# Linear attention and two MLP layers on one core: attention by whole load groups, tail key products over 128 rows, rms_g inside the gate and value weights

## The chip, the cores and the metric

The kernel runs on one core of a Trainium2 chip. The metric is device time in microseconds (us), from the start of the execution to its end. One execution was also recorded by the hardware profiler; its span is the time from the first to the last instruction that the profiler saw. The engines are named as in the profile: PE is the matrix engine, PEld its weight loads, DVE the vector engine, ACT the scalar engine, POOL the GpSimd engine, and SP the engine that issues the transfers.

## The reference

Three layers follow one another. The inputs are four batches, eight heads, 576 positions of 64 values, 128 random features, and three weight pairs.

```python
scale = 1.0 / np.sqrt(np.sqrt(D))
def phi(x):
    proj = np.einsum('bhsd,md->bhsm', x, omega)
    sq = np.sum(x * x, axis=-1, keepdims=True) / 2.0
    h = proj - sq
    h = h - np.max(h, axis=-1, keepdims=True)
    return np.exp(h) / np.sqrt(m)
q_p, k_p = (phi(q * scale), phi(k * scale))
kv = np.einsum('bhsm,bhsd->bhmd', k_p, v)
z = np.sum(k_p, axis=2)
x = num / den                      # num = q_p @ kv, den = q_p @ z + 1e-6, as [2304, 512]

xn = x / np.sqrt(np.mean(x * x, -1, keepdims=True) + 1e-06) * rms_g
g = xn @ w_gate                    # 512 -> 1536
x = (g / (1 + np.exp(-g))) * (xn @ w_val) @ w_out

h = x @ w_in                       # 512 -> 2048
out = (h / (1 + np.exp(-h))) @ w2_out
```

## The kernel before

**Numbers in two parts.** Every product that needs more than one pass keeps its operands as a high and a low part, and adds three products (PASS). The weights arrive as 64-bit numbers: `w_decode` turns them into 32 bits, with five steps on DVE (lines 156 to 167) and two integer additions on POOL (line 170, `w_add`); ACT then writes the high part (line 180) and DVE the low one (line 183).

**Attention.** A load brings 256 positions of four heads (a "load group", `add_load`) or, for the last 64 positions of two batches together, one half-size tail group. POOL squares and halves it (lines 545, 549), and DVE reduces it to norms (line 558). A unit of work (`add_unit`) is half a load group, that is two heads, or one tail group: two 128x128 transposes on PE into half a PSUM bank (line 586), high part by ACT (592), low part by DVE (595), six products with omega of 256 columns each (605), the maxima on DVE (620), two small DVE instructions for the bias (626, 633), four exponentials on ACT (644). There are 64 half groups and 8 tail groups, 72 units in all. A key unit ends in eight products of 64 output rows by 65 columns into the accumulator `kv` (690). A tail group of keys holds two batches in its upper and lower 64 rows, so its products run over 64 rows, four of them at the end of the even batch and four at the end of the odd one. The finished `kv` is copied by DVE (710, `kvs`). A query unit ends in four transposes (721), a copy by ACT (727), eight products with `kvs` (736, for tails 742), and denominator, reciprocal and quotient on DVE (759, 762, 772).

**Norm and transposes.** For each 128 positions ACT sums squares (803), POOL takes the root (814, 817), DVE multiplies by it and by `rms_g` in one instruction (833, tile `g_sb`, a copy of the vector in every row), PE transposes (842), ACT and DVE split (851, 856) into the tile `xs`.

**What sets the order.** Everything up to the third block of tokens of the first sweep is planned by `run_order`: each step is an `Op` with engine, duration, wanted slots and a priority, to which the table `RANK` adds a number by kind; `SLOTS` gives the number of buffers. Slot kind `b` is six PSUM banks. The first sweep of the gated layer covers two of twelve feature blocks: its six weight tiles are gated by `pj_ops[24 + 2 * n]`, the projections of units 24 to 34, and its products are `part` (line 236) and `out` (963) for the first three blocks of 512 tokens. Three weight tiles of the second sweep also belong to the plan.

**The stream.** After the plan, `stream` writes the rest in a fixed order: products of gate and value (236, tile `g`), output products (290, 323, tile `y`). `Prep.tick` puts one weight load, the decoding of the weight loaded before, the high part of the one before that and the low part of the one before that between them, each time that 3.2 us (until the second sweep's weights are there), later 5.5 us, of PE work by its own count has been written.

## Time and profile before

| | before |
|---|---|
| median of three runs | 1011.57 us (1009.81 to 1011.66) |
| the profiled execution, its own time | 1011.63 us |
| its span | 1009.8 us |
| PE busy | 992.4 us (98%), granted clock 0.998 |
| DVE, ACT, POOL busy | 587.8, 374.6, 282.2 us (58%, 37%, 28%) |

The profiled execution is 0.06 us from the median; 1.83 us of its time lie outside the span. A busy PE need not be a PE at its peak: a matmul is counted from its start to its modelled end, and the next can start before that end. The share of DVE and ACT over the whole span hides that nearly all of attention lies in the first 167 us, where both are close to full.

### The profile page before, as it was taken

The numbers are of one execution on the slowest core, as the hardware profiler recorded it, in microseconds if no ns is written. First come the engines' busy times: TensorE is split into PE (matmuls) and PEld (weight loads), VectorE is DVE, ScalarE is ACT, GpSimd is POOL, SyncE is SP. The second block draws the span as 40 slices with busy tenths as digits, with TensorE's granted clock in tenths as the row PEclk, the third lists the DMA queues.
The fourth block names the chain that finished last, engine by engine and source line by source line (L and its number), as shares of the span: only waits on it lengthen the run. The fifth ranks groups of instructions, "written<-read, shape, count | busy, mean of one in ns | idle before, by whom it ended". The sixth has DMA issues, their size and how long they took to land.

```text
span 1009.8 us, 15330 instructions
## 1 busy us (share of the span) xinstructions
PE 992.4 (98%) x5935; PEld 842.4 (83%) x5935; DVE 587.8 (58%) x1289; ACT 374.6 (37%) x861; POOL 282.2 (28%) x287
## 2 busy tenths in 40 slices
PE   7999998999999999999999999999999999999998
PEld 7988886788888888888888888888888888888887
DVE  7899998837852345676332776443654544535633
ACT  6988895344221112222111334433322322322321
POOL 6756632415520002344000231321411411201300
PEclk9999999999999999999999999999999999999999
DMA  7444211212320002222000120210210210200023
GB/s 196 123 122 131 67 30 42 64 41 84 104 63 1 1 1 64 63 85 83 21 1 1 42 63 22 84 42 5 79 42 6 78 42 22 63 1 21 21 84 105
DMA packets 68729, 55.85 MB, mean 55 GB/s; under 512 B 25648, under 2 KB 62768, under 8 KB 68656
## 3 DMA queue, kind: packets, MB, share of 16 engines
q1 hardware_dynamic: 68656, 54.87, 18.4%
q8 instruction: 47, 0.77, 0.3%
q14 instruction: 26, 0.21, 0.1%
HBM read 50.14 MB, written 4.72 MB: 54 GB/s over the span
## 4 chain that ended last, share of the span: by engine, by line
PE 89%; DVE 7%; issue 1%; POOL 1%; ACT 1%; DMA 1%; SPq 0%; DVEq 0%; ACTq 0%; POOLq 0%
PE g L236 43%; PE y L323 19%; PE y L290 12%; PE b L605 4%; PE b L236 3%; PE kv L690 2%; DVE small L620 2%; PE b L963 2%; PE b L736 1%; PE b L721 1%; PE b L586 1%; DVE hl L595 1%; DVE w L183 1%; POOL m L170 1%; DVE xt L833 1%
## 5 line engine op out<-in xcount | busy, mean ns | idle before, releaser
L236 PE MATMUL g<-xs,w 128*128 128x512 f32 (+1 forms) x2256 | 467.9, 366 | 0.0
L236 PEld LDWEIGHTS g<-xs,w 128*128 128x128 f32 x2256 | 391.2, 188 | 70.1
L170 POOL TENSOR_TENSOR m<-m,raw 128x512 int32<-128x512 int32 x136 | 189.9, 1396 | 612.6 <-issue 442.6
L230 DVE TENSOR_TENSOR h<-s,h 128x512 fp32r<-128x512 f32 (+1 forms) x134 | 96.0, 717 | 185.0 <-ACT h L229 185.0
L323 PE MATMUL y<-w,h 128*128 128x512 f32 (+1 forms) x870 | 200.8, 388 | 0.0
L323 PEld LDWEIGHTS y<-w,h 128*128 128x128 f32 x870 | 162.2, 188 | 33.3
L229 ACT ACTIVATE h<-s 128x512 fp32r<-128x512 f32 (+1 forms) x134 | 78.7, 588 | 191.5 <-DVE s L259 169.5
L290 PE MATMUL y<-h,w 128*128 128x512 f32 (+1 forms) x648 | 135.6, 366 | 0.3 <-DVE w L183 0.3
L290 PEld LDWEIGHTS y<-h,w 128*128 128x128 f32 x648 | 112.1, 189 | 20.5 <-DVE w L183 0.8
L270 ACT ACTIVATE s<-g 128x512 f32<-128x512 f32 (+1 forms) x80 | 44.4, 556 | 171.0 <-PE g L236 170.9
L334 DVE TENSOR_TENSOR ya<-y,ya 128x512 f32<-128x512 f32 (+1 forms) x91 | 62.2, 684 | 57.8 <-PE y L323 56.5
L259 DVE TENSOR_TENSOR s<-s,g 128x512 f32<-128x512 f32 (+1 forms) x54 | 33.8, 627 | 84.8 <-PE g L236 84.8
L301 DVE TENSOR_TENSOR ya<-y,ya 128x512 f32<-128x512 f32 (+1 forms) x80 | 50.2, 635 | 54.3 <-PE y L290 54.1
L180 ACT ACTIVATE w<-m 128x512 fp32r<-128x512 f32 x68 | 42.7, 628 | 102.8 <-POOL m L170 102.8
L644 ACT ACTIVATE e<-b,nb 128x128 f32<-128x128 f32 x272 | 77.5, 395 | 3.7 <-DVE nb L633 3.6
L605 PE MATMUL b<-bd,hl 128*128 128x256 f32 x432 | 69.5, 300 | 1.7 <-DVE hl L595 1.1
L605 PEld LDWEIGHTS b<-bd,hl 128*128 128x128 f32 x432 | 56.8, 192 | 5.4 <-DVE hl L595 2.3
L620 DVE TENSOR_REDUCE small<-b 128x4 f32<-128x512 f32 x72 | 50.2, 697 | 6.2 <-PE b L605 2.2
L253 ACT ACTIVATE s<-g 128x512 f32<-128x512 f32 (+1 forms) x54 | 29.7, 550 | 64.1 <-PE g L236 63.9
L183 DVE TENSOR_TENSOR w<-m,w 128x512 fp32r<-128x512 f32 x68 | 52.9, 779 | 0.1
L545 POOL TENSOR_TENSOR sq<-x 128x512 f32<-128x512 f32 (+1 forms) x40 | 38.9, 982 | 36.2 <-DMA x<-in_q_dram 9.8
L549 POOL TENSOR_TENSOR sq<-sq 128x256 f32<-128x256 f32 (+2 forms) x80 | 44.4, 573 | 2.3
(69 smaller groups left out, 739.7 us busy)
## 6 DMA issues: line engine op xcount, KB each, us to landing
raw<-in_moe_w_out_dram SPq DMA_DIRECT2D x28, 512.0 KB, 3.5
raw<-in_moe_w_in_dram SPq DMA_DIRECT2D x16, 512.0 KB, 3.7
raw<-in_moe_w_gate_dram SPq DMA_DIRECT2D x12, 512.0 KB, 3.6
raw<-in_moe_w_val_dram SPq DMA_DIRECT2D x12, 512.0 KB, 3.5
x<-in_k_dram SPq DMA_DIRECT2D x16, 256.0 KB, 3.4
va<-in_v_dram SPq DMA_DIRECT2D x32, 128.0 KB, 3.3
x<-in_q_dram SPq DMA_DIRECT2D x16, 256.0 KB, 3.0
out_dram<-ya SPq DMA_DIRECT2D x15, 256.0 KB, 2.0
```

The lines of the kernel that those rows point to most:

```text
L170: tt(out=mi, in0=mi, in1=(low if step == 5 else high).bitcast(I32), op=ALU.add)
L183: nc.vector.tensor_tensor(out=st.t[:, 1, :], in0=st.m.bitcast(F32), in1=st.t[:, 0, :].bitcast(F32), op=ALU.subtract)
L229: nc.scalar.activation(out=ht[:, 0, :], in_=s, func=AF.Copy)
L230: nc.vector.tensor_tensor(out=ht[:, 1, :], in0=s, in1=ht[:, 0, :].bitcast(F32), op=ALU.subtract)
L236: nc.tensor.matmul(out=ps, lhsT=w[:, a, cc * P:(cc + 1) * P], rhs=xs[j][:, c, cc, :], start=(n == 0), stop=(n == 3 * KC - 1),)
L290: nc.tensor.matmul(out=ps, lhsT=wt[1, "o", f][:, a, d * P:(d + 1) * P], rhs=hs[f][:, c, :], start=(n == 0), stop=(n == nn - 1),)
L301: nc.vector.tensor_tensor(out=y[:, d, :], in0=ps, in1=y[:, d, :], op=ALU.add)
L323: nc.tensor.matmul(out=ps, lhsT=hs[f][:, a, t * P:(t + 1) * P], rhs=wt[2, "p", f][:, c, d0:d1], start=(n == 0), stop=(n == nn - 1),)
L334: nc.vector.tensor_tensor(out=o[:, t, d0:d1], in0=ps, in1=o[:, t, d0:d1], op=ALU.add)
L605: nc.tensor.matmul(out=st.ps[:, 2 * j:2 * j + 2, :].rearrange("p h m -> p (h m)"), lhsT=st.hl[:, c, j, :], rhs=bd[:, a, :], start=(n == 0) ...
L620: nc.vector.tensor_reduce(out=st.mx, in_=st.ps, axis=AX.X, op=ALU.max)
L644: nc.scalar.activation(out=st.e[:, h, :], in_=st.ps[:, h, :], func=AF.Exp, bias=st.nb[:, h:h + 1])
```

## The change

- **Whole load groups.** A unit is now one load group. Its four transposes go into one whole bank, one high part and one low part cover 512 columns, the bias instructions cover eight columns at a time. The projections, maxima and exponentials still come in halves, each half with its own bank. There are 40 units: 32 whole and 8 tails. A whole group's sixteen key products, or its two sets of query products, are placed one behind the other.
- **Tails.** The values of a tail are loaded for one batch at a time into a tile whose other 64 rows POOL has filled with zeros (`pad`), so that the tail's products run over all 128 rows in the form of the other products.
- **kvs** is copied by ACT instead of DVE.
- **rms_g.** `g_sb` now holds one number for each row and chunk; POOL multiplies the gate and value weights by it in a third POOL instruction. DVE multiplies the tokens by the root alone, with a one-tensor instruction. All 24 gate and value weights get the third instruction; the output weights and the second layer's don't.
- **Planner.** `RANK` has its own numbers for queries and keys; the first sweep's weights are gated by units 3 to 8 of 40. `SLOTS`: x 5 to 4, hl 3 (of half size) to 2 (of whole size), e 3 to 4, nmc 1 to 2.

```diff
-        else:
+        elif step < 7:
             mi = st.m.bitcast(I32)
             tt(out=mi, in0=mi, in1=(low if step == 5 else high).bitcast(I32), op=ALU.add)
+        else:
+            mf = st.m.bitcast(F32).rearrange("p (c f) -> p c f", c=KC)
+            tt(out=mf, in0=mf, in1=g_sb.rearrange("p (c o) -> p c o", o=1).to_broadcast([P, KC, P]), op=ALU.mult)
+
+    def scaled(job):
+        return job[2][1] in "gv"
...
-                    for s in range(7):
+                    for s in range(8 if scaled(job) else 7):
...
+        "pad": -346.8, "ld_vt": -10.6, "ld_om": -43.4, "t_om": 133.7, "s_om": -176, "bd_hi": -101,
...
+    def add_tail_v(u, i, e, prev):
+        kind, b, hf, g = u
+        t = va_tail[g]
+
+        def pad(o):
+            nc.gpsimd.memset(t[64 - 64 * e:P - 64 * e], 0.0)
+            nc.gpsimd.memset(t[64 * e:64 * e + 64, :, :, D:D + 1], 1.0)
...
+            st.pt = buf(ps_a, [P, 2 * R, P], "b", o.slot["b"])
+            st.hl = buf(wk, [P, 2, 4, P], "hl", o.slot["hl"], F32R)
+            for j in range(2 * R):
+                nc.tensor.transpose(st.pt[:, j, :], flat()[:, j * P:(j + 1) * P], ident)
...
+            def maxima(o, r=r):
+                if r == 0:
+                    n = o.slot["nb"]
+                    st.mx, st.top = small[:, n, 0:G * R], small[:, n, 2 * G:2 * G + G * R]
+                    st.nb = buf(wk, [P, G * R], "nb", n)
+                nc.vector.tensor_reduce(out=st.mx[:, G * r:G * r + G], in_=st.ps[r], axis=AX.X, op=ALU.max)
...
-                nc.vector.tensor_copy(out=acc.sb, in_=acc.ps)
-
-            kvcopy[b, g] = Op("kvs", "DVE", 0.34, copy, [o], i, ["kvs"], [(acc.op, "kv")])
+                nc.scalar.activation(out=acc.sb, in_=acc.ps, func=AF.Copy)
+
+            kvcopy[b, g] = Op("kvs", "ACT", 0.31, copy, [o], i, ["kvs"], [(acc.op, "kv")])
...
+    def add_tail(b, g, e, i, st, ex, vop, pad, free):
+        def jobs():
+            return [(h, st.e[0][:, h, :], va_tail[g][:, h, 0, :]) for h in range(G)]
...
-            nc.vector.scalar_tensor_tensor(
-                out=st.x, in0=st.x, scalar=xs_.rstd[:, r:r + 1], in1=g_sb, op0=ALU.mult, op1=ALU.mult
+            nc.vector.tensor_scalar(
+                out=st.x, in0=st.x, scalar1=xs_.rstd[:, r:r + 1], scalar2=None, op0=ALU.mult
             )
...
-        g_op = Op("ld_g", "SP", 1.0, lambda o: nc.sync.dma_start(out=g_sb, in_=rms_g.partition_broadcast(P)), prio=8)
+        g_op = Op("ld_g", "SP", 1.0, lambda o: nc.sync.dma_start(out=g_sb, in_=rms_g.rearrange("(c p) -> p c", p=P)), prio=8)
...
-            add_weight(job, n, [pj_ops[24 + 2 * n]])
+            add_weight(job, n, [pj_ops[GATE + n]])
```

PE in the middle of attention, where queries of batch 0 alternate with keys of batch 1. In a row, the tile left of the arrow is written from those right of it; `hl` are the split transposes, `e` the exponentials, `kv` and `kvs` accumulator and its copy, `qT` the turned query features. Before:

```order
L605 MATMUL b_881<-bd,hl_735 128x256 x6
L586 MATMUL b_898<-ident,x_603 128x128 x2
L605 MATMUL b_902<-bd,hl_817 128x256 x6
L586 MATMUL b_920<-ident,x_492 128x128 x2
L721 MATMUL b_925<-ident,e_891 128x128 x4
L605 MATMUL b_936<-bd,hl_834 128x256 x6
L586 MATMUL b_949<-ident,x_603 128x128 x2
L690 MATMUL kv_744<-va_101,e_861 64x65 x8
L690 MATMUL kv_744<-vat_102,et_358 128x65 x4
L736 MATMUL b_982<-kvs_648,qT_857 64x65 x8
L721 MATMUL b_1004<-ident,e_972 128x128 x4
```

And now:

```order
L626 MATMUL b_900<-bd,hl_802 128x256 x6
L626 MATMUL b_916<-bd,hl_802 128x256 x6
L694 MATMUL kv_685<-va_101,e_791 64x65 x8
L694 MATMUL kv_685<-va_101,e_831 64x65 x8
L694 MATMUL kv_685<-vat_102,et_330 64x65 x8
L777 MATMUL b_967<-kvs_434,qT_898 64x65 x8
L777 MATMUL b_979<-kvs_434,qT_909 64x65 x8
L694 MATMUL kv_996<-va_99,e_926 64x65 x8
L694 MATMUL kv_996<-va_99,e_948 64x65 x8
L605 MATMUL b_1025<-ident,x_758 128x128 x4
```

The small products (65 columns) stand in longer runs between the wide ones, and the tail row has the form of the others: eight products of 64 output rows instead of four of 128. Over the whole plan such runs number 39 before and 25 now.

PE where the first products of the gated layer appear (`w_0` is the gate weight of the first feature block, `xs_90` the first 512 tokens, `xt` the tokens before their transposes). Before:

```order
L736 MATMUL b_3177<-kvs_2916,qT_3086 64x65 x8
L721 MATMUL b_3188<-ident,e_3137 128x128 x4
L721 MATMUL b_3199<-ident,e_3170 128x128 x4
L236 MATMUL b_3211<-xs_90,w_0_1833 128x512 x6
L721 MATMUL b_3226<-ident,e_3205 128x128 x4
L236 MATMUL b_3211<-xs_90,w_0_1833 128x512 x3
```

And now:

```order
L752 MATMUL b_1758<-ident,e_1722 128x128 x4
L242 MATMUL b_1766<-xs_90,w_0_1019 128x512 x3
L626 MATMUL b_1772<-bd,hl_1728 128x256 x6
L626 MATMUL b_1784<-bd,hl_1728 128x256 x6
L242 MATMUL b_1766<-xs_90,w_0_1019 128x512 x9
L605 MATMUL b_1825<-ident,x_1595 128x128 x2
```

Before, the first such product stood behind the last projection of attention; now 36 of the 48 that the first 512 tokens take stand between the projections of batches 1 to 3.

POOL where the plan ends and the stream begins (`m` is a weight being decoded, `ss` and `rstd` belong to the norm). Before:

```order
L170 TENSOR_TENSOR m_3539<-m_3539,raw_3504 128x512 x2
L170 TENSOR_TENSOR m_3607<-m_3607,raw_3553 128x512 x2
L814 TENSOR_SCALAR ss_3716<-ss_3716 128x1
L817 TENSOR_TENSOR rstd_3717<-ss_3716,mhalf 128x1
L170 TENSOR_TENSOR m_3815<-m_3815,raw_3781 128x512 x2
L170 TENSOR_TENSOR m_3883<-m_3883,raw_3823 128x512 x2
```

And now:

```order
L170 TENSOR_TENSOR m_3320<-m_3320,raw_3275 128x512 x2
L173 TENSOR_TENSOR m_3320<-m_3320,g_sb 128x512
L852 TENSOR_SCALAR ss_3531<-ss_3531 128x1
L855 TENSOR_TENSOR rstd_3532<-ss_3531,mhalf 128x1
L170 TENSOR_TENSOR m_3626<-m_3626,raw_3592 128x512 x2
L173 TENSOR_TENSOR m_3626<-m_3626,g_sb 128x512
L170 TENSOR_TENSOR m_3695<-m_3695,raw_3635 128x512 x2
L173 TENSOR_TENSOR m_3695<-m_3695,g_sb 128x512
```

Each gate or value weight has one more POOL instruction of the same shape behind its two additions.

## Rows read from the trace of the kernel before

**Rows 1.** Windows: stretch, length, busy time and instructions by engine, clock, DMA share, GB/s.

```profile
30.00:140.00 110.00, 106.95 (x1401) 97.13 (x1402) 102.72 (x349) 97.27 (x321) 69.97 (x103) 1.00 0.37 98
140.00:167.00 27.00, 21.70 (x230) 17.85 (x229) 23.33 (x64) 20.24 (x56) 7.74 (x10) 0.94 0.13 40
264.30:1006.30 742.00, 741.93 (x3538) 625.02 (x3538) 371.10 (x678) 195.75 (x344) 145.36 (x104) 1.00 0.14 42
```

**Rows 2.** Chain that ended last, in order of time: start, us, what.

```profile
47.28 0.71 PE b L605 x6
...
61.32 0.44 PE b L721 x4
61.76 0.62 PE kv L690 x16
62.38 0.47 PE b L736 x16
62.85 0.93 PE b L605 x6
...
77.99 1.03 PE kv L690 x8
```

**Rows 3.** The same chain where the stream takes over.

```profile
218.18 13.73 PE g L236 x72
...
242.36 3.52 DMA raw<-in_moe_w_out_dram
...
264.32 6.66 PE y L290 x28
270.98 16.32 PE g L236 x72
```

**Rows 4.** DVE and ACT groups to 218 us: line, shapes, count, busy, mean ns, idle.

```profile
L620 DVE TENSOR_REDUCE small<-b 128x4 f32<-128x512 f32 x72 | 50.2, 697 | 6.2 <-PE b L605 2.2
L595 DVE TENSOR_TENSOR hl<-b,hl 128x256 fp32r<-128x256 f32 x72 | 29.4, 418 | 1.1 <-ACT hl L592 0.6
L833 DVE SCALAR_TENSOR_TENSOR xt<-xt,rstd,g_sb 128x512 f32<-128x512 f32 x18 | 15.4, 879 | 1.8 <-POOL rstd L817 1.7
L856 DVE TENSOR_TENSOR xs<-b,xs 128x512 fp32r<-128x512 f32 x18 | 12.0, 682 | 2.3 <-ACT xs L851 2.2
L626 DVE SCALAR_TENSOR_TENSOR small<-ns,small 128x4 f32<-128x4 f32 x72 | 11.5, 160 | 0.6
L162 DVE TENSOR_SCALAR m<-m 128x512 f32<-128x512 f32 x9 | 3.7, 413 | 0.0
L710 DVE COPY kvs<-kv 128x260 f32<-128x260 f32 x8 | 3.4, 424 | 0.1
L644 ACT ACTIVATE e<-b,nb 128x128 f32<-128x128 f32 x272 | 77.5, 395 | 3.7 <-DVE nb L633 3.6
L592 ACT ACTIVATE hl<-b 128x256 fp32r<-128x256 f32 x72 | 28.6, 404 | 9.3 <-PE b L586 8.7
L851 ACT ACTIVATE xs<-b 128x512 fp32r<-128x512 f32 x18 | 10.8, 602 | 2.7 <-PE b L842 2.3
```

**Rows 5.** Timeline of SP, which issues the transfers, in the first microseconds.

```profile
1.23 0.49 SPq L1015 DMA_DIRECT2D om<-in_omega_dram  x1
1.76 0.47 SPq L488 DMA_DIRECT2D x<-in_k_dram  x1
```

**Rows 6.** Timeline of POOL early in the stream: start, us, engine, line, shapes, count, idle.

```profile
239.65 2.69 POOL L170 TENSOR_TENSOR m<-m,raw 128x512 int32<-128x512 int32 x2 [1.42 <-ACT s L253]
...
260.69 3.02 POOL L170 TENSOR_TENSOR m<-m,raw 128x512 int32<-128x512 int32 x2 [2.49 <-issue]
```

**Rows 7.** Timeline of DVE in the same stretch.

```profile
247.00 1.53 DVE L159 TENSOR_SCALAR raw<-raw 128x512 uint32<-128x512 uint32 x1
...
262.48 1.79 DVE L183 TENSOR_TENSOR w<-m,w 128x512 fp32r<-128x512 f32 x1
```

**Rows 8.** Windows, projections (line 605) alone: PE and its weight loads.

```profile
30.00:140.00 110.00, 50.47 (x317) 41.02 (x318) 1.00 0.37 98
```

More of the change, by code (lines that the diff above doesn't have):

```diff
@@ L613, in add_unit @@
[L613 to L623 removed]
+        st.ps, st.e, pjs, mxs, exs = {}, {}, [], [], []
@@ new lines, in add_unit, with project @@
+        for r in range(R):
+            def project(o, r=r):
+                st.ps[r] = buf(ps_a, [P, G, P], "b", o.slot["b"])
+                for j in range(2):
+                    for n, (a, c) in enumerate(PASS):
+                        nc.tensor.matmul(
+                            out=st.ps[r][:, 2 * j:2 * j + 2, :].rearrange("p h m -> p (h m)"),
+                            lhsT=st.hl[:, c, 2 * r + j, :],
+                            rhs=bd[:, a, :],
+                            start=(n == 0),
+                            stop=(n == 2),
+                        )
+            last = r == R - 1
+            pj = Op("pj." + kind[0], "PE", 0.715, project, [lo] + bd_ops, i, ["b", "pjc"], [(tr, "hl")] if last else [])
+            pjs.append(pj)
+            def maxima(o, r=r):
[4 more added lines that the diff above has]
+                nc.vector.tensor_reduce(out=st.mx[:, G * r:G * r + G], in_=st.ps[r], axis=AX.X, op=ALU.max)
+            mxs.append(Op("mx." + kind[0], "DVE", 0.64, maxima, [pj] + mxs, i, ["nb"] if r == 0 else []))
@@ L624, in add_unit @@
+        pj_ops.append(pjs[0])
         top = Op(
-            "top", "DVE", 0.13,
+            "top." + kind[0], "DVE", 0.11,
             lambda o: nc.vector.scalar_tensor_tensor(
-                out=st.top, in0=st.ns, scalar=half, in1=st.mx, op0=ALU.mult, op1=ALU.add
+                out=st.top, in0=w.ns, scalar=half, in1=st.mx, op0=ALU.mult, op1=ALU.add
             ),
-            [mx, w.nsop], i,
+            mxs + [w.nsop], i,
         )
         nb = Op(
-            "nb", "DVE", 0.13,
+            "nb." + kind[0], "DVE", 0.11,
@@ L633, in add_unit @@
             lambda o: nc.vector.scalar_tensor_tensor(
[L634 removed]
+                out=st.nb, in0=w.ns, scalar=half, in1=st.top, op0=ALU.mult, op1=ALU.subtract
             ),
[L636 removed]
+            [top], i, free=[(w.sqop, "ns")],
         )
         res = f"et{g}" if kind == "kt" else "e"
[L640 to L646 removed]
@@ L648, in add_unit, with exps @@
-        ex = Op("ex", "ACT", 1.004, exps, [nb], i, [res], [(pj, "b"), (pj, "pjc"), (mx, "nb")])
+        for r in range(R):
+            def exps(o, r=r):
+                pool = kp if kind == "kt" else wk
+                st.e[r] = buf(pool, [P, G, M], res, o.slot[res])
+                for h in range(G):
+                    nc.scalar.activation(
+                        out=st.e[r][:, h, :], in_=st.ps[r][:, h, :], func=AF.Exp,
+                        bias=st.nb[:, G * r + h:G * r + h + 1],
+                    )
+            exs.append(Op(
+                "ex." + kind[0], "ACT", 1.004, exps, [nb], i, [res],
+                [(pjs[r], "b"), (pjs[r], "pjc")] + ([(mxs[0], "nb")] if r == R - 1 else []),
+            ))
@@ L672, in add_kv, with add_products @@
+            num = None
+            for r in range(R):
+                num = add_q(u, i, st, r, evs, num)
+    def add_products(b, g, i, jobs, deps, first, end, dur, free):
         acc = kvfirst.setdefault((b, g), State())
@@ L676, in accumulate @@
                 acc.ps = buf(ps_a, [P, G, D + 1], "kv", o.slot["kv"])
[L677 to L689 removed]
+            todo = jobs()
+            for n, (h, lhsT, rhs) in enumerate(todo):
+                for c in HALVES:
                     nc.tensor.matmul(
@@ L727, in evac, with add_q @@
-            nc.scalar.activation(out=st.qt, in_=st.pe, func=AF.Copy)
-        ev = Op("ev", "ACT", 0.478, evac, [fl], i, ["qT"], [(fl, "b")])
+            st.e[r] = buf(wk, [P, G, P], "qT", o.slot["qT"])
+            nc.scalar.activation(out=st.e[r], in_=pe[0], func=AF.Copy)
+        return Op("ev", "ACT", 0.495, evac, [fl], i, ["qT"], [(fl, "b")])
+    def add_q(u, i, whole, half_unit, evs, prev):
+        kind, b, hf, g = u
+        tail = kind == "qt"
+        hp = 2 * g + half_unit
+        st = State()
+        ev = evs[half_unit]
@@ L790, in add_q, with spot @@
                 add_norm(i, key, r, r == R - 1)
+        return num
+    def spot(key, r):
+        kind, b, hf = key
+        j, n = divmod(tidx["m" if kind == "q" else "t", b, hf, r], TB)
+        return j, n * P
     def add_norm(i, key, r, last):
```

243 lines of the change are left out of this document (99 added, 144 removed), and 8 rows, old and new, of tables (RANK, SLOTS).

## Prediction

> **What bounds the kernel now.** The windows by stage come first, since shares over the whole span mix stages with different limits. From 264.3 to 1006.3 us PE is busy for 741.93 of 742.00 us [rows 1]: nothing that DVE, ACT or POOL save there can change the end, and the change takes no PE work out of that stretch. The kernel can be won or lost ahead of it. From 30 to 140 us PE is busy 106.95 of 110 us, DVE 102.72 (93%) and ACT 97.27 (88%) [rows 1]. Three engines near full mean that the busy share of PE cannot be believed, as it counts matmuls that overlap. So I rebuild PE's work from the chain of waits, whose pieces leave the overlap out.
>
> Six projections take 0.71 us, four transposes 0.44, the small products of one half group 0.47 when they follow other small products and 0.62 when they follow a transpose, a projection behind small products 0.93 instead of 0.71, and a tail's products 1.03 [rows 2]. A wide product of the gated layer takes 16.32/72 = 0.227 us [rows 3]. Up to 218.18 us, where the stream takes over [rows 3], the plan holds: 72 sets of projections, 51.1 us; 360 transposes, 39.6; 32 key and 36 query sets of small products at 0.47, 32.0; 8 tails, 8.2; 39 runs of small products, each with 0.15 on entering and up to 0.22 on leaving (I take 0.30 together), 11.7; 216 wide products, 49.0. The sum is 191.6 us, so PE stands idle for about 26.6 us of the 218.2. These 26.6 us, and what becomes cheaper in the 191.6, are all there is to gain. The stretch from 140 to 167 us has its part in them: PE is busy 21.70 of 27.00 there, and its granted clock of 0.94 says that a little of it ran at the lower of its two levels [rows 1].
>
> **The change part by part.** *PE.* Eight tails go from 1.03 to the 0.47 us of the form that they now take: -4.5. Fourteen of 39 runs of small products vanish: 14 x 0.30 = -4.2. Together -8.7 us, on the engine that is nearest to being the bound. If DVE or ACT is late instead, part of it becomes idle time: between 0 and 8.7 of it arrives, and I take all of it, because DVE becomes lighter too.
>
> *DVE.* The low parts of the split go from 72 x 0.418 to 32 x 0.682 (the same operation on 512 columns) and 8 x 0.418: -4.9. The bias instructions go from 144 to 80, of 0.160: -10.2. The norm's product with two tensors, 18 x 0.879, becomes a one-tensor instruction, nearest to the row of 0.413: -8.4. The copy of `kvs` leaves: -3.4 [rows 4]. That is 26.9 us of row durations; the maxima stay. DVE has 93% in the middle stretch, so this is where it would pay by itself; but PE is close behind and takes over.
>
> *ACT.* The high parts go from 72 x 0.404 to 32 x 0.602 + 8 x 0.404, -6.6; `kvs` comes, 8 x 0.424 by DVE's row [rows 4], +3.4. ACT sheds 3.2 us in all, so it is the engine that the others now run into.
>
> *Filling PE's gaps.* The order puts 36 wide products, 36 x 0.227 = 8.2 us, between the projections of batches 1 to 3. They must run some time; put into gaps they cost nothing, put into a full stretch they only move. So this is worth between 0 and 8.2 us. I take 3.0, nearer to the lower end, because ACT is at 88% in that stretch [rows 1] and the two feature blocks bring it work as well. The six weights must be decoded earlier for that, which adds no instruction, but moves some DVE and POOL work into the fuller part; DVE's -26.9 covers it, and without this cover each weight would cost about five times 0.41 and one 0.68.
>
> *Start.* The load of omega is issued third instead of second: 1.76 - 1.23 = 0.53 us later [rows 5]; the first split covers 512 columns instead of 256, 0.602 - 0.404 on ACT and 0.682 - 0.418 on DVE [rows 4], 0.46 us. The first projection comes up to 1.0 us later, of which I take 0.7, between 0 and 1.0: the pieces behind it have slack among themselves.
>
> *POOL.* Each gate or value weight gets a third instruction; the nearest row is the addition of the same shape, 2.69/2 = 1.35 us [rows 6]. Of 24, seven lie in the plan, three in the rush at the start of the stream, fourteen later, where PE never waits and POOL is busy 145.36 of 742 us [rows 1]: they cost nothing, and up to 1.1 us each (1.53 - 0.41, below) if PE did wait for a weight there. In the rush it is different. The last output weight of the second sweep ends on DVE at 264.27, and PE starts on it at 264.32 [rows 3, 7]: there is no slack. That weight's way goes back through DVE to a load issued at 242.36, which waited for a buffer that POOL's additions had held [rows 3, 6]. DVE is held up beside a POOL instruction: L159 took 1.53 us beside one, while a DVE instruction of this kind alone takes 0.41; L183 took 1.79 [rows 4, 7]. The three weights before the output weights are all gate or value weights, so three more POOL instructions stand in front of that load and in DVE's way. The price lies between 0 (in POOL's idle times of 1.42 to 2.49 us [rows 6]) and 3 x 1.35 = 4.1; I take 2.0, since the idle time of 1.42 just fits one and the DVE instructions beside it still wait. Behind DVE's waiting instruction stand the gated product and the low part of the hidden values, and for them PE's output products.
>
> The zero fills of the tails are POOL writes of 260 columns on half the rows, sixteen small instructions in all, far ahead of use; POOL has 40 of 110 us free in the middle stretch [rows 1]. The load of `g_sb`, now of single numbers, is waited for only by the first third instruction, a long way behind. Both at nothing. If POOL were full they would delay the norms.
>
> The sum: -8.7 - 3.0 + 0.7 + 2.0 = -9.0 us. The profiled execution took 1011.63 us, 1.83 of it outside its span, and stands at the median of 1011.57; so 1002.6.
>
> **The rivals.** *ACT becomes the bound* of the middle stretch. For it: 88% already, and it sheds least. If it gets no further than 90%, the stretch holds (97.27 - 2.1)/0.90 = 105.7 us and shrinks by 4.3 instead of the 8.9 that its share of the PE savings (two thirds, 5.9) and the filling would give. Then 4.6 us are missing: 1007.2. Against it: in the stretch DVE itself reached 93%.
>
> *DVE was the bound throughout*, and its 26.9 us set everything free: the filling brings its 8.2, the stretch from 140 to 167 us another 3, the rush costs only 1.0: -8.7 - 8.2 - 3.0 + 0.7 + 1.0 = -18.2, 993.4. For it: the 93%. Against it: PE itself has only 26.6 us of idle time, and the start and the last queries keep most of theirs, being chains of dependent steps.
>
> *Whole groups wait longer (slower).* The first exponential of a group now waits for the maxima of both halves, one more maximum of 0.697 us [rows 4], and a group's query products wait for both copies. With 32 whole groups that is 22.3 us at the most, if nothing else covers it. It decides from 9.0/32 = 0.28 us per group on; at 0.5 us per group the time is 1002.6 + 16 = 1018.6. For it: four banks for projections hold two groups instead of four halves. Against it: two groups in flight are enough as long as one holds its banks for less than twice the 4.2 us that a group takes now (the stretch of 110 us holds 317 projections, so 53 halves [rows 8]), and the steps (two projections 1.4, a second maximum 0.7, two bias instructions 0.3, eight exponentials at 77.5/272 each, 2.3 [rows 2, 4]) add up to some 4.7.
>
> *POOL locks DVE out more widely.* Rows: above, 1.53 against 0.41. If every third instruction in plan and rush holds DVE for its full 1.35 us, four weights of the first sweep in attention and three in the rush, it is 9.5 instead of the 2.0 that I counted: 1010.1. The Trainium skill ("SBUF — State Buffer", "Who interferes with whom") calls the ports that VectorE and GpSimd share an exclusive lock, which whoever issues first keeps for its whole instruction. The rows agree, 1.53 us in place of 0.41; by the rule alone all seven products would cost their full length, the 1010.1, and by POOL's idle times the sum stays at 1002.6.
>
> *It does nothing to the end:* what PE saves turns into waiting for loads or norms. 1011.6 plus or minus 1.
>
> **How the numbers follow.** The forecast has a chance of 0.45, ACT 0.20, DVE 0.12, whole groups 0.12, the lock 0.05, nothing 0.06. A difference of 0.2%, 2 us, is about what a measurement of this kernel can tell from no change. Faster by more: forecast, ACT and DVE, 0.77, to which I add 0.01 for the lock's lighter half; within: 0.10; slower: 0.12. The forecast's own terms, at their ends, give 1011.6 - 8.7 - 8.2 = 994.7, and 1011.6 - 4.4 + 1.0 + 4.1 = 1012.3 with half of the PE savings lost. The range runs from 993, the DVE case, to 1011 and leaves out the slow group case and the top of the bounds.
>
> **What would show it.** Right: the stream starts near 207 us instead of 218.2; a tail's products at 0.47 us; the norm's product near 0.41; ACT above 90% in the middle stretch, DVE clearly below its 93%; 36 wide products before the last projection; PE waiting 2 us or so for an output weight of the second sweep. Wrong: a stream that starts at 215 or later with PE idle behind exponentials (ACT), or behind bias instructions (whole groups); PE waits behind weights after 270 us, which would break the assumption that the stream covers POOL; loads that come late, since two weights of 512 KB now stand early among the loads of keys and queries.

## The result and the profile after

| | before | after |
|---|---|---|
| median of four runs | 1010.93 us (1009.81 to 1011.66) | 1000.03 us (999.15 to 1000.13) |
| span of the profiled execution | 1009.8 us | 998.1 us |
| first wide product of the stream on PE | 218.0 us | 204.9 us |

The ratio is 0.9891, interval 0.9874 to 0.9908. The forecast was 1002.6, in a range of 993 to 1011: the sign, the range and nearly the size held. The time was gained ahead of the stream, 13.1 us, of which some 1.4 were lost behind its start, 1.2 of them in the rush. How it was gained is another matter, and most of what follows is about that.

Part of it is TensorE's clock. Some fifty executions of the kernel before that were timed beside the experiments took 1008.9 to 1010.4 us where the mean granted clock was 0.999 or more, and 1010.4 to 1012.3 where it was 0.998 or less. In the profiled one (1011.63) PE paused for 1.54 us before 155.23, and then the granted clock was 0.50, the lower of the two levels, for some 3.4 us, all of the stretch from 156 to 158 us among them. At half the rate that is at most 1.7 us of work. The changed kernel's profile shows no such drop ahead of its stream, so up to 1.7 of the 13.1 us go with the clock.

The windows of the kernel after answer to [rows 1] (stretch, its length, then PE, PEld, DVE, ACT, POOL with their instructions, granted clock, DMA share, GB/s):

```profile
30.00:140.00 110.00, 105.50 (x1482) 97.57 (x1482) 104.15 (x285) 98.72 (x303) 82.15 (x122) 1.00 0.39 103
140.00:167.00 27.00, 25.12 (x293) 22.13 (x288) 23.91 (x72) 23.45 (x70) 11.42 (x13) 1.00 0.19 59
252.46:994.60 742.14, 742.05 (x3538) 624.94 (x3538) 377.19 (x678) 196.63 (x344) 161.43 (x118) 1.00 0.14 42
```

In the middle stretch DVE did not fall below its 93%, as the prediction wanted to see: it stands at 104.15 of 110, 95%, though it has less to do in all. POOL went from 64 to 75%, and ACT stands at 90%. From 140 to 167 us PE does 25.12 us of work where it did 21.70, at the full clock. In the stream PE is busy for all but 0.09 us of 742, although POOL has 16 us more to do there.

The groups of the kernel after to 205 us answer to [rows 4] (line, engine, shapes, count, busy us, mean ns, idle before):

```profile
L643 DVE TENSOR_REDUCE small<-b 128x4 f32<-128x512 f32 x72 | 50.0, 695 | 5.7 <-PE b L626 3.2
L614 DVE TENSOR_TENSOR hl<-b,hl 128x512 fp32r<-128x512 f32 x32 | 21.8, 683 | 2.2 <-ACT hl L610 1.9
L871 DVE TENSOR_SCALAR xt<-xt,rstd 128x512 f32<-128x512 f32 x18 | 10.5, 609 | 1.7 <-POOL rstd L855 1.7
L162 DVE TENSOR_SCALAR m<-m 128x512 f32<-128x512 f32 x9 | 5.0, 551 | 0.0
L656 DVE SCALAR_TENSOR_TENSOR nb<-ns,small 128x8 f32<-128x8 f32 x32 | 5.0, 156 | 0.5
L668 ACT ACTIVATE e<-b,nb 128x128 f32<-128x128 f32 x272 | 76.9, 400 | 4.4 <-DVE nb L656 2.7
```

The norm's product (L871) takes 0.609 us in the mean, not 0.41. The weights' step L162, which took 0.413 before, takes 0.551: five of the nine weights are now worked on ahead of 140 us, beside a fuller POOL.

### The profile page after: what moved, and what is told of

The parts are those of the page before. It is cut to its first block, busy times and chain, and to the rows that moved or that the text cites. A ratio compares the mean times of both kernels' runs of the same rounds, so it can differ in the third digit from the quotient of the medians.

```text
span 998.1 us, 15350 instructions
## 1 busy us (share of the span) xinstructions
PE 980.1 (98%) x5999; PEld 836.3 (84%) x5999; DVE 582.7 (58%) x1185; ACT 372.0 (37%) x837; POOL 314.4 (32%) x325
## 4 chain that ended last, share of the span: by engine, by line
PE 87%; DVE 8%; ACT 3%; issue 1%; DMA 0%; SPq 0%; DVEq 0%; ACTq 0%
PE g L242 43%; PE y L329 20%; PE y L296 12%; PE b L626 3%; PE b L242 3%; PE b L1001 2%; DVE small L643 1%; ACT e L668 1%; PE b L777 1%; PE kv L694 1%; DVE w L189 1%; PE b L752 1%; DVE hl L614 1%; PE b L605 1%; DVE m L156 1%
## 5 line engine op out<-in xcount | busy, mean ns | idle before, releaser
L235 ACT ACTIVATE h<-s 128x512 fp32r<-128x512 f32 (+1 forms) x134 | 78.7, 588 | 183.6 <-DVE s L265 161.7
L186 ACT ACTIVATE w<-m 128x512 fp32r<-128x512 f32 x68 | 42.8, 629 | 117.2 <-POOL m L170 68.9
L668 ACT ACTIVATE e<-b,nb 128x128 f32<-128x128 f32 x272 | 76.9, 400 | 4.4 <-DVE nb L656 2.7
L626 PE MATMUL b<-bd,hl 128*128 128x256 f32 x432 | 65.6, 299 | 3.9 <-DVE hl L614 2.8
L189 DVE TENSOR_TENSOR w<-m,w 128x512 fp32r<-128x512 f32 x68 | 55.6, 817 | 0.0
L259 ACT ACTIVATE s<-g 128x512 f32<-128x512 f32 (+1 forms) x54 | 29.5, 547 | 58.7 <-PE g L242 58.6
L558 POOL TENSOR_TENSOR sq<-sq 128x256 f32<-128x256 f32 (+2 forms) x80 | 46.5, 600 | 1.6
```

The costliest lines, as they stand in the source:

```text
L189: nc.vector.tensor_tensor(out=st.t[:, 1, :], in0=st.m.bitcast(F32), in1=st.t[:, 0, :].bitcast(F32), op=ALU.subtract)
L235: nc.scalar.activation(out=ht[:, 0, :], in_=s, func=AF.Copy)
L626: nc.tensor.matmul(out=st.ps[r][:, 2 * j:2 * j + 2, :].rearrange("p h m -> p (h m)"), lhsT=st.hl[:, c, 2 * r + j, :], rhs=bd[:, a, :], sta ...
L668: nc.scalar.activation(out=st.e[r][:, h, :], in_=st.ps[r][:, h, :], func=AF.Exp, bias=st.nb[:, G * r + h:G * r + h + 1],)
```

## The experiments

Twelve kernels ran; all but one are edits of the changed kernel. Start is PE's first wide product of the stream in the one profiled execution, time the median. The profiled execution need not lie at the median: that of d1 is its fastest, 1.0 us below, that of e3 its slowest, 0.7 above, and d3 and e2, whose edits leave the plan's order alone, start at 204.8 and 204.4. So the two columns are to be read together. All are to be held against 204.9 and 1000.03, except for b1_norm, which is an edit of the kernel before (218.0; 1010.70 measured beside it).

| run | what it changes | start | time (lowest to highest) |
|---|---|---|---|
| e9_wide_out | PE 7.5 us lighter: 33 of 36 wide products left out | 203.6 | 999.13 (998.87 to 999.46) |
| d1_no_norm | DVE 10.5 us lighter: norm's products left out | 201.1 | 997.40 (996.37 to 997.77) |
| d3_short_squares | ACT 6.5 us lighter: squares over 64 of 512 columns | 204.8 | 1000.02 (998.97 to 1000.22) |
| d2_both | the first two together | 201.8 | 997.63 (997.11 to 997.82) |
| e3_tail64 | tails undone | 207.4 | 1002.93 (1002.12 to 1003.61) |
| e4_bias_halves | bias instructions undone | 207.5 | 1003.24 (1002.69 to 1004.17) |
| b1_norm | norm's product alone, rms_g left out | 214.0 | 1007.82 (1007.12 to 1008.32) |
| e1_gate14 | another order | 215.0 | 1010.13 (1006.73 to 1013.01) |
| e7_turn3 | another order | 205.8 | 1000.88 (1000.57 to 1001.12) |
| e5_om_second | omega loaded second | 203.6 | 998.20 (997.51 to 998.92) |
| e2_no_third | third instruction left out in rush and stream | 204.4 | 997.91 (997.68 to 998.33) |
| v1_om_rush | e5, and the rush paced faster | 201.9 | 1007.77 (1006.94 to 1008.83) |

### One part undone

**e3_tail64**, the tails' products over 64 rows again, four for a tail, each with all 128 output rows. The changed kernel has eight over 128 rows, in two column halves; the expectation has the halves and the counts the wrong way round.

```diff
-                for c in HALVES:
+                for c in HALVES if lhsT.shape[0] == P else [slice(0, P)]:
...
-            return [(h, st.e[0][:, h, :], va_tail[g][:, h, 0, :]) for h in range(G)]
+            return [(h, st.e[0][64 * e:64 * e + 64, h, :], va_tail[g][64 * e:64 * e + 64, h, 0, :]) for h in range(G)]
```

> The changed kernel with one part undone: the key products of the eight tails run over 64 rows in two column halves again (16 small products per tail instead of 8 over 128 rows); all else, the order of instructions too, stays as in the changed kernel. Theory (PE's own work sets the time up to the stream): a tail's products go from 0.47 back to about 1.03 us in the chain of waits, the stream starts about 8 x 0.56 = 4.5 us later than the 205.0 us of the changed kernel, near 209.5, and the whole time is near 1004.5. Rival (DVE was the bound and its relief made the gain): PE has room beside a DVE that is 95% busy in the middle stretch, so the start of the stream moves by 0 to 1 us and the time stays within 1000 to 1001.

The chain of waits shows the size of the term to the hundredth. Each small product leaves two rows in the profile. In the changed kernel a whole group (16 products, 32 rows) with a tail (8 products, 16 rows) takes 1.55 us, and two whole groups with a tail 2.49:

```profile
47.81 1.55 PE kv L694 x48
...
124.29 2.49 PE kv L694 x80
```

and in e3 the same work, whose tail has 4 products, 8 rows:

```profile
48.13 2.12 PE kv L694 x40
...
125.59 3.05 PE kv L694 x72
```

0.57 and 0.56 us for each tail, 4.5 for eight, as predicted from [rows 2]. But the stream starts 2.5 us later and the time is 2.9 higher: a little over half arrives. The theory is right that it arrives, not that all of it does.

**e4_bias_halves**, two bias instructions for each one. The cut shows the second of the two (`nb`); the first (`top`) is split in the same way.

```diff
...
-            lambda o: nc.vector.scalar_tensor_tensor(
-                out=st.nb, in0=w.ns, scalar=half, in1=st.top, op0=ALU.mult, op1=ALU.subtract
-            ),
+            lambda o: [nc.vector.scalar_tensor_tensor(
+                out=st.nb[:, G * r:G * r + G], in0=w.ns[:, G * r:G * r + G], scalar=half,
+                in1=st.top[:, G * r:G * r + G], op0=ALU.mult, op1=ALU.subtract
+            ) for r in range(R)],
```

> The changed kernel with one part undone: each bias instruction of DVE over a whole group is issued as two over a half each again, 64 more instructions at about 0.16 us, 10 us more on DVE up to the stream, nothing else. Theory (PE sets the time, DVE's relief only covers): the stream starts 0 to 4 us later than 205.0, the time is between 1000 and 1004. Rival (DVE sets the time in the middle stretch, where it is 95% busy): nearly all of the 10 us arrives, 7 to 10 us, and the time is 1007 to 1010, so that the kernel has lost most of its gain over the one before.

The time is 3.2 us higher, the start 2.6 later: inside the theory's 0 to 4. But what came in was less than both theories put in. Windows to the start of the stream, of the changed kernel and then of e4:

```profile
0.00:204.90 204.90, 191.80 (x2226) 172.22 (x2227) 169.06 (x451) 158.45 (x462) 128.79 (x190) 1.00 0.37 99
```

```profile
0.00:207.50 207.50, 191.35 (x2226) 171.10 (x2227) 173.35 (x515) 158.70 (x462) 128.46 (x190) 1.00 0.37 98
```

64 more instructions make DVE 4.3 us busier, where 64 rows of 0.16 would be 10.2. Not all of the difference is theirs. The bias instructions' own rows cover 20.0 us in place of 12.7, 7.3 more or 0.11 each, while the weights' six steps on DVE (L156 to L167 and L189), some of which run beside POOL, cover 30.1 in place of 32.5. Why 0.11 and not 0.16, the timeline of DVE in the changed kernel shows:

```profile
40.11 0.15 DVE L656 SCALAR_TENSOR_TENSOR nb<-ns,small 128x8 f32<-128x8 f32 x1
40.18 0.28 DVE L567 TENSOR_REDUCE ns<-sq 128x8 f32<-128x128 f32 x1
```

The next instruction starts 0.07 us after this one, inside its 0.15: a row's duration is not the time for which it keeps others out. The Trainium skill (Perfetto Trace Analysis, "Optimizing Scalar/DVE Operations") says that the profiled latency of a DVE instruction's data access is about twice the time for which it keeps the engine busy; 0.07 of 0.15 agrees. It does not hold for each pair: in e4 two such instructions in a row take 0.22 us, but two of the other bias instruction (L649) take 0.35. Of the 4.3 us of DVE time 2.6 arrive, again over half.

**b1_norm**, the kernel before with the norm's product alone.

```diff
-            nc.vector.scalar_tensor_tensor(
-                out=st.x, in0=st.x, scalar=xs_.rstd[:, r:r + 1], in1=g_sb, op0=ALU.mult, op1=ALU.mult
+            nc.vector.tensor_scalar(
+                out=st.x, in0=st.x, scalar1=xs_.rstd[:, r:r + 1], scalar2=None, op0=ALU.mult
```

> The kernel before with one part of the change alone: the norm's product as a one-tensor instruction on DVE, without rms_g, which is thereby left out of the result (no third instructions on POOL either). 18 instructions go from 0.88 to 0.6 us, 5 us less on DVE, nothing else; the order stays. Theory (PE's own work sets the time up to the stream and DVE is only close behind): the stream starts 0.5 to 2 us earlier than the 218.2 of the kernel before, the time is 1009 to 1010.5. Rival (DVE sets the time): 4 to 5 us earlier, the time is near 1006. Rival (all hidden): within 0.5 us of the kernel before.

DVE's busy time to the stream falls by 5.0 us (183.77 to 178.78), the start by 4.0, the time by 2.9 (ratio to the kernel before 0.9973, 0.9963 to 0.9984). By the start this looks like the rival that let DVE set the time. But the profiled execution of the kernel before has the drop of the clock, up to 1.7 us, and that of b1 has none. Of the executions of the kernel before that were timed beside b1, the five at a clock of 0.999 or more took 1009.14 to 1010.28, the middle one 1009.71: against these b1 is 1.9 us faster. So the edit itself brings some two microseconds, the upper end of the theory: in the kernel before, a microsecond of DVE's work was worth some 0.4 to 0.5.

### Each engine lighter

**e9_wide_out**, one product left of each of the first three sets of twelve.

```diff
+                        if j == 0 and (nm, f) in (("g", 0), ("v", 0), ("g", 1)):
+                            if c0 == 0:
+                                nc.tensor.matmul(
+                                    out=st.p[nm], lhsT=wt[1, nm, f][:, 0, :P], rhs=xs[j][:, 0, 0, :],
+                                    start=True, stop=True,
+                                )
+                            return
                         part(wt[1, nm, f], j, st.p[nm], c0, c0 + GRAIN)
```

> The changed kernel without 33 of the 36 wide products that stand between the projections (of each of the first three sets of twelve only one is left); this leaves out part of the first gate and value products, and nothing else changes, the order included. The 33 are 7.5 us of PE's work. Theory (they fill gaps that PE would have waited in, about 3 of 8 us of them): the stream starts 3.5 to 5.5 us earlier than 205.0, so 2 to 4 us of the work was free. Rival (they only moved, PE is full where they stand): 7 to 7.5 us earlier. Rival (they stand wholly in gaps, as DVE, 95% busy there, sets the pace): 0 to 1.5 us earlier.

The theory that PE's own work sets the time falls here. 7.5 us of products vanish, the start moves by 1.3 and the time by 0.9. The middle stretch of e9:

```profile
30.00:140.00 110.00, 100.02 (x1467) 92.43 (x1463) 104.67 (x287) 98.94 (x307) 82.19 (x122) 1.00 0.39 102
```

PE is idle for 5.5 us more in the same stretch, and DVE and ACT are as full as they were. So the wide products stand almost wholly in gaps: what I valued at 3.0 of 8.2 us was worth nearly all of it.

**d1_no_norm**, **d3_short_squares** and **d2_both** (e9 and d1 in one kernel).

```diff
-            nc.vector.tensor_scalar(
-                out=st.x, in0=st.x, scalar1=xs_.rstd[:, r:r + 1], scalar2=None, op0=ALU.mult
-            )
```

```diff
-            junk = xs[j][:, 1, :, o0:o0 + P]
-            nc.scalar.activation(out=junk, in_=xs_.x[:, r].rearrange("p (c a) d -> p c (a d)", c=KC), func=AF.Square, accum_out=xs_.ss[:, r:r + 1])
+            junk = xs[j][:, 1, :, o0:o0 + 16]
+            nc.scalar.activation(out=junk, in_=xs_.x[:, r].rearrange("p (c a) d -> p c (a d)", c=KC)[:, :, 0:16], func=AF.Square, accum_out=xs_.ss[:, r:r + 1])
```

> The changed kernel without the norm's products on DVE (the factor 1/rms of each row is left out of the result). PE's work and every order stay; DVE loses 18 instructions, 10.5 us, 9.1 us of them between 60 and 167 us. It is the counterpart to the run without 33 wide products, in which PE lost 7.5 us and the stream started only 1.3 us earlier. Theory after that run (DVE sets the pace in the middle stretch, where it is 95% busy): the stream starts 4 to 7 us earlier than 204.9, the time is 993 to 996. Rival (the prediction's own: PE's content sets the time): 0 to 1.5 us earlier, 998.5 to 1000. Rival (ACT and the steps of a group are just behind DVE): 1.5 to 3.5 us earlier.

> The changed kernel with the squares of the norm on ACT taken over 64 of 512 columns, which leaves most of the sum of squares out of the result. Every order stays; ACT loses some 7 us (18 instructions from 0.66 to about 0.27), about 5.5 of them between 60 and 167 us, DVE and PE lose nothing. It is the third of a set: PE lighter by 7.5 us gave 0.9 us, DVE lighter by 10.5 us gave 2.6. Rival of the prediction (ACT is what the others run into in the middle stretch): the stream starts 3 to 5.5 us earlier than 204.9, the time is 995 to 997. Theory after the runs so far (DVE's instructions pace the groups, ACT follows them): the stream starts 0 to 1.5 us earlier, 998.5 to 1000. Rival (the engines are linked so tightly that relief on any of them arrives in part): 1.5 to 3 us earlier.

> The two omissions together: the changed kernel without the norm's products on DVE and without 33 of the 36 wide products between the projections, so that DVE has 10.5 and PE 7.5 us less work. Theory (DVE sets the pace, PE has room): as without the norm's products alone, and up to 2 us more, since PE comes close behind a lighter DVE: the stream starts 4 to 9 us earlier than 204.9. Rival (PE and DVE are level, and each holds the other): the two together bring much more than the sum of the two alone, 7 us or more, while each alone brought little. Rival (ACT or the steps of a group): no more than the better of the two alone, 1.5 to 3.5 us.

DVE lighter by 10.5 us starts the stream 3.8 us earlier; just short of the theory's 4 to 7, and by the time (2.6 us) between the theory and the rival of ACT and the steps. ACT lighter by 6.5 us (158.45 to 151.99 up to the stream) does nothing at all, so the rival with ACT as the bound falls: its 90% were slack. The two together measured no better than d1 alone. That doesn't settle whether their gains add up, for d2's granted clock was 0.50 from 98 to 101 us, in which up to 1.7 us were lost, and all four executions have a mean clock of 0.998; without that loss d2 could lie near the sum of the two. The middle stretch of d1, and of d3:

```profile
30.00:140.00 110.00, 107.10 (x1506) 99.63 (x1505) 100.04 (x285) 100.38 (x310) 80.58 (x122) 1.00 0.39 101
```

```profile
30.00:140.00 110.00, 105.53 (x1484) 97.60 (x1484) 104.06 (x285) 94.83 (x303) 81.47 (x121) 1.00 0.40 103
```

In d1 all three engines have gaps and PE does 1.6 us more. The chain of waits tells the same. Its pieces between 30 and 167 us, summed by engine: PE 76 and DVE 43 of 137 us in the changed kernel, PE 69 and DVE 48 without the wide products, PE 97 and DVE 19 without the norm's products, PE 57 and DVE 65 with halved bias instructions. The end goes over from one to the other: with less work on one, the other's steps are what is left. (The ACT share is no evidence: 13 us in the changed kernel and 4 in d3, with the same start; where two paths end together, the chain shows either.) What limits d2, where PE, DVE and ACT are all below 95% in the middle stretch, the runs don't settle; the sequence of steps in a group remains, and it wasn't tried.

### The order

```diff
-    W_EARLY, GRAIN, GATE = 3, 3, 3
+    W_EARLY, GRAIN, GATE = 3, 3, 14
```

> The changed kernel with one number of the planner's changed (GATE 14 instead of 3), so that the wide products of the gated layer come later: 24 instead of 36 stand ahead of the last projection, and these 24 begin at the 212th group of TensorE instructions instead of the 129th. The planner orders some other work anew as well. Theory (the wide products fill gaps of PE between the projections): the stream starts 1 to 4 us later than 205.0 and the time is 1001 to 1004. Rival (the wide products only move, no gap is filled): within 1 us of 1000. If the decoding of weights in the middle of attention costs more than the filling brings, it is faster than 1000 by a microsecond or two.

```diff
-    PE_SLOW, TURN = 8.5, 0.12
+    PE_SLOW, TURN = 8.5, 0.08
```

> The changed kernel with the planner's price of a switch to small products lowered from 0.12 to 0.08: another order of the same instructions, with the same 25 runs of small products, but with 12 instead of 36 wide products ahead of the last projection. Theory (runs of small products and filled gaps matter, not the order by itself): 24 wide products, 5.4 us, lose their gaps; the stream starts 1 to 4 us later than 205.0, the time is 1001 to 1004. Rival (the wide products are worth nothing where they stand): within 1 us of 1000. Rival (the order that the planner happened to find is a large part of the gain): more than 5 us later, above 1005, as in the run with the gate at 14.

The same instructions in another order give back the whole gain in e1 (ratio 1.0, 0.9989 to 1.0012) and almost none of it in e7 (0.9907, 0.9892 to 0.9922), although only 12 wide products stand ahead of the last projection in e7, and 24 in e1. So the number of wide products there is not the measure: the theory misses e1 by six microseconds, a part of which is the clock's (below), and e7 goes with the rival for which they are worth nothing where they stand, since that order finds other work for the gaps (PE is busy 105.72 of 110 us in its middle stretch). What e1 does show is work that came late. Windows of e1 and of the changed kernel:

```profile
140.00:167.00 27.00, 22.31 (x245) 20.07 (x243) 23.50 (x60) 18.45 (x55) 10.82 (x13) 0.94 0.13 41
167.00:200.00 33.00, 32.46 (x218) 26.74 (x219) 28.95 (x62) 14.88 (x30) 15.06 (x14) 1.00 0.17 51
```

```profile
140.00:167.00 27.00, 25.12 (x293) 22.13 (x288) 23.91 (x72) 23.45 (x70) 11.42 (x13) 1.00 0.19 59
167.00:200.00 33.00, 33.00 (x204) 27.11 (x203) 20.46 (x45) 14.64 (x28) 12.74 (x11) 1.00 0.16 50
```

DVE has 28.95 us to do after 167 us where the changed kernel has 20.46 (four of its weights begin there, not two), and PE waits at the end of attention, as it did before the change [rows 1], at the same granted clock of 0.94. The waits of e1 between 100 and 175 us (line, releaser, us, times, longest) name DVE:

```profile
PE b L777 <- DVE nb L656: 2.4, 1, 2.4
PE b L777 <- DVE small L649: 2.2, 1, 2.2
PE b L777 <- DVE hl L614: 1.7, 1, 1.7
```

Some of e1's ten microseconds are the clock's. Behind a pause of PE of 2.43 us its granted clock was 0.50 from 154 to 157 us. Of its twelve executions the only one at a mean clock of 1.0 took 1006.73 us, the five at 0.998 took 1009.49 to 1009.95, the five at 0.994 took 1012.38 to 1013.01. So the order by itself costs nearer to 6.7 us, by that one execution. That the late weights cause these is argued, not shown; the planner moved other work as well.

### Start and rush

```diff
-        "pad": -346.8, "ld_vt": -10.6, "ld_om": -43.4, "t_om": 133.7, "s_om": -176, "bd_hi": -101,
+        "pad": -346.8, "ld_vt": -10.6, "ld_om": -45.5, "t_om": 133.7, "s_om": -176, "bd_hi": -101,
```

> The changed kernel with one rank of the planner's changed, so that the load of omega is issued second instead of third, as in the kernel before; PE's order stays but for some 36 lines at the start. In the changed kernel PE waits 5.3 us for omega (4.0 before) and does its first full projection 2.3 us later than before. Theory (the late omega is what the start costs): PE waits 4.0 to 4.5 us for omega, and the stream starts 0.7 to 2 us earlier than 205.0; the time is 998 to 999.3. Rival (the start is covered by slack behind it, or the first split over 512 columns and not omega is what is late): within 0.5 us of 1000.

The first rows of PE in the changed kernel, and in e5 (start, us, engine, line, shapes, count, idle before):

```profile
5.28 0.45 PE L1035 MATMUL b<-ident,om 128*128 128x128 f32 x1 [5.28 <-DMA om<-in_omega_dram]
5.52 1.91 PE L605 MATMUL b<-ident,x 128*128 128x128 f32 x8
7.39 0.58 PE L626 MATMUL b<-bd,hl 128*128 128x256 f32 x1
8.30 2.71 PE L626 MATMUL b<-bd,hl 128*128 128x256 f32 x11 [0.33 <-DVE hl L614]
```

```profile
4.10 0.45 PE L1035 MATMUL b<-ident,om 128*128 128x128 f32 x1 [4.10 <-DMA om<-in_omega_dram]
4.34 1.06 PE L605 MATMUL b<-ident,x 128*128 128x128 f32 x4
5.83 1.12 PE L605 MATMUL b<-ident,x 128*128 128x128 f32 x4 [0.43 <-DMA x<-in_k_dram]
6.60 2.30 PE L626 MATMUL b<-bd,hl 128*128 128x256 f32 x12
```

In the kernel before, omega was there at 4.01 us:

```profile
4.01 0.45 PE L997 MATMUL b<-ident,om 128*128 128x128 f32 x1 [4.01 <-DMA om<-in_omega_dram]
```

One place in SP's queue costs it 1.2 us and the projections 1.7. The time falls by 1.8 us, the start by 1.3; in v1, which has the same plan, by 3.0. The theory holds, and e5 is faster than both kernels: 0.988 of the kernel before (0.9866 to 0.9893), its slowest run below the fastest of the changed kernel.

```diff
-                    for s in range(8 if scaled(job) else 7):
+                    for s in range(7):
```

> The changed kernel without the third instruction (the multiplication by rms_g on POOL) for the weights that are decoded after the planned part; this leaves that factor out for all but the first sweep's weights. Theory (the third instructions cost only in the rush behind the start of the stream, where PE waits for an output weight of the second sweep): the stream starts at 205.0 as before, PE's first output product of the second sweep comes about 46.2 us later instead of 47.4, the wait of 1.21 us for the weight shrinks to 0.3 or less, and the time is 1.0 to 1.3 us lower, near 998.9. Rival (POOL's instructions hold up DVE and through it PE all along the stream): more than 2 us lower. Rival (the waiting weight is set by its load and not by POOL): within 0.3 us of 1000.

PE's waits behind the start, of the changed kernel and then of e2 (line, releaser, us, times, longest):

```profile
PE y L296 <- DVE w L189: 1.2, 1, 1.2
```

```profile
PE y L296 <- DVE w L189: 0.3, 1, 0.3
```

PE's wait for the output weight shrinks from 1.2 to 0.3 us, and that product comes 46.3 us after the start, as in the kernel before [rows 3], instead of 47.6. The time falls by 2.1 us. The rush explains 1.2 of it, the theory's mechanism at the price that it named. The start is 0.5 us earlier, although the edit leaves the plan as it is, so this half microsecond is the difference between two executions.

```diff
-    W_PACE, W_RUSH = 5.5, 3.2
+    W_PACE, W_RUSH = 5.5, 2.5
```

> An attempt at a better version: the changed kernel with omega loaded second again (998.2 by itself) and the weights of the second sweep worked on sooner in the rush (W_RUSH 2.5 instead of 3.2). Theory (PE's wait of 1.2 us for the output weight comes from the pace of the weights' work on DVE and POOL): the wait shrinks to 0.3 or less and the time is about 997.2. Rival (the wait is set by POOL's third instructions and by the load behind them, whatever the pace): the wait stays near 1.2, the time at 998.2. Rival (the weights' work now stands in front of the gated products and low parts): PE waits more, 999 or above.

The second rival, that the weights' work now stands in front, is right, and by far more than it said. The timeline of ACT in v1:

```profile
231.44 0.63 ACT L186 ACTIVATE w<-m 128x512 fp32r<-128x512 f32 x1 [3.91 <-POOL m L170]
231.97 0.37 ACT L259 ACTIVATE s<-g 128x256 f32<-128x256 f32 x1
235.81 0.63 ACT L186 ACTIVATE w<-m 128x512 fp32r<-128x512 f32 x1 [3.48 <-POOL m L170]
236.35 0.40 ACT L235 ACTIVATE h<-s 128x256 fp32r<-128x256 f32 x1
```

and that of PE:

```profile
229.09 0.51 PE L296 MATMUL y<-h,w 128*128 128x256 f32 x3
236.80 4.81 PE L296 MATMUL y<-h,w 128*128 128x256 f32 x21 [7.20 <-ACT h L235]
```

The faster pace puts a weight's high part (L186) ahead of a step of the hidden value on ACT, once before L259 and once before L235. Each time the weight waits for POOL (3.91 and 3.48 us), the hidden value stands behind it, and PE waits 7.2 us for the result. (A high part that waits for POOL ahead of L259, for 3.48 us, stands in the changed kernel too, where PE doesn't wait; the one ahead of L235 is new.) Work that is offered early is work that others stand behind.

## Why the prediction came out, step by step

**PE.** The tails' 0.47 us is right to the hundredth, and 2.5 to 2.9 of 4.5 us arrive (e3). The 14 runs fell away as counted (39 to 25), but no run took them alone; their 4.2 us are open. The step that failed is "I take all of it, because DVE becomes lighter too": PE's work arrives by half when it grows, and by a sixth when it shrinks (e9).

**DVE.** The term of 26.9 us was a sum of row durations. DVE's busy time up to the stream fell by 14.7 (183.77 to 169.06). Three things make up the 12 us between. The norm's product saves 4.9 by its rows instead of 8.4. The weights' six steps grew from 30.4 to 32.5 us and the low part of the hidden value (L977) from 4.1 to 5.3, beside a fuller POOL. The rest, some five, is rows that overlap: 64 bias instructions cover 7.3 us in e4, where I had 10.2. The norm's product reaches its short form only when POOL leaves it alone: the ten of its 18 instructions that run beside no POOL instruction take 0.474 to 0.486 us, the eight others 0.487 to 1.232. The Trainium skill (SBUF — State Buffer, "Who interferes with whom") counts this form among those that can take the port pair shared with GpSimd; the spread agrees. So a part of DVE's 95% is time in which POOL held it up. And the sum gave DVE's relief nothing of its own, since "PE is close behind and takes over". That was too low: by start or time a DVE microsecond is worth some 0.4 to 0.5 in the kernel before (b1, without the clock's part), 0.2 to 0.4 (d1) and 0.6 to 0.7 (e4) in the changed one. The rival "DVE was the bound throughout" was nearer on this; what kept the time from its 993.4 is that DVE lost 14.7 us and not 26.9, and that PE does take over (its pieces of the chain rise from 76 to 97 us in d1).

**ACT.** That others run into it is refuted by d3. I had read 88% as a limit from its share alone.

**Filling.** Mis-sized: 3.0, measured nearly all of the 7.5 us taken out in e9. Taking a small part of the price "because ACT is at 88%" was the same error.

**Start.** Mis-sized: 0.7 with 1.0 as the upper end; e5 and v1 put omega's place alone at 1.3 (e5, with a drop of the clock, see the last section) to 3.0 (v1, without). I counted the 0.53 us between two rows of SP's timeline [rows 5], but omega landed 1.3 us later, and everything behind it.

**POOL.** Right in place and mechanism, 1.2 us by e2 against 2.0. The third instruction took 1.05 us in the median, where the row of the addition gave 1.35. Later in the stream the third instructions cost nothing, as said: 742.05 of 742.14.

**Whole groups.** Didn't come: ACT stood idle 4.4 us in all ahead of its 272 exponentials (L668 above), 2.7 of them behind the bias, about as before [rows 4].

So the sum came near because errors had both signs: too much for PE's work and DVE's, too little for the filling and the start. Of the 13.1 us at the start the runs account for the tails (2.5), the bias instructions (2.6) and the norm's product with the clock's drop (4.0, measured in the kernel before), less 1.3 to 3.0 for omega. The remaining five to seven have the size that e9 gives to the filling (6.2 of 7.5 us in gaps), but e7 takes two thirds of the filling away for 0.9. So the filling, the whole-bank splits, `kvs`, the runs and the order itself were not taken apart, and e1 shows that the order alone can be worth nearly seven.

## What to carry to other kernels

Where two engines hand work to each other at 95%, ask what a microsecond is worth on each by taking some out and putting some in: here it was 0.1 to 0.6 on PE, 0.2 to 0.7 on DVE, nothing on ACT, and no busy share told that. Price an engine's work by the start-to-start distance of its rows, not by their durations. And when a planner sets the order, vary one of its numbers first: its luck can be most of the change.

## What was not expected of the hardware

**Behind the same short pause PE's clock fell in one run and not in another.** e5 and v1 have the same plan and nearly the same pause of PE behind DVE, from about 12.2 us on. In e5 the granted clock was 0.50 from 15 to 18 us, the lower of the two levels, and the next small products show it:

```profile
13.90 0.66 PE L605 MATMUL b<-ident,x 128*128 128x128 f32 x4 [1.70 <-DVE hl L614]
...
15.59 2.00 PE L694 MATMUL kv<-va,e 128*64 128x65 f32 x32
```

In v1 it was 1.00, the higher:

```profile
13.72 0.66 PE L605 MATMUL b<-ident,x 128*128 128x128 f32 x4 [1.57 <-DVE hl L614]
...
15.02 1.16 PE L694 MATMUL kv<-va,e 128*64 128x65 f32 x32
```

e5's runs come in two sorts by it, 997.5 to 997.7 at a mean clock of 1.0 and 998.8 to 998.9 at 0.998. The kernel before, e1 and d2 show the same drop behind pauses of 1.54 and 2.43 us and behind two of 0.83 and 0.86 within two microseconds. And behind the 7.2 us pause of v1, which ends at 236.80, the granted clock is 0.84 from 236 to 252 us, which adds to that pause. What decides between the two outcomes no run here shows.
